# Attention in periods of six units, with one block of value products a group, in a kernel of hash attention and two mixers

## The chip, the cores and the metric

The kernel runs on 1 core of one Trainium2 chip. The metric is the device time of one execution in microseconds, the median of three runs. Engines are named TensorE (PE in the profile, with PEld for its weight loads), VectorE (DVE), ScalarE (ACT), GpSimd (POOL) and SyncE (SP, which only issues DMAs here).

## The reference, cut to what matters

Attention over 2 batches, 8 heads, 768 positions and 64 channels a head, in which a query sees only the keys of its hash bucket. Two mixing networks follow it; the change does not touch them.

```python
q_bits = (np.einsum('bhsd,dk->bhsk', q, proj) > 0).astype(np.int64)
k_bits = (np.einsum('bhsd,dk->bhsk', k, proj) > 0).astype(np.int64)
...
mask = q_bucket[:, :, :, None] == k_bucket[:, :, None, :]
scores = scale * np.matmul(q, k.transpose(0, 1, 3, 2))
scores = np.where(mask, scores, -1000000000.0)
scores = scores - np.max(scores, axis=-1, keepdims=True)
attn = np.exp(scores)
attn = attn / (np.sum(attn, axis=-1, keepdims=True) + 1e-09)
return np.matmul(attn, v).astype(np.float32)
```

## The kernel before

**Tiling.** A unit is 128 queries of one head against all 768 keys; there are 96 (`nunits`). A group is six units, three query tiles of each of the two heads of a head pair for half of the positions; there are 16. A pair is two groups; there are 8 (`npairs`). Units are numbered 0 to 95 through the whole kernel; where a unit is called 0 to 5 it is counted within its group.

**A unit's steps.** `scores` (L326, TensorE): four products of 128x384 into a tile `s` in PSUM, of which there are two. `peak` (L336, VectorE): moves `s` to SBUF (`p`, three buffers) and takes the row's maximum; `bias` (L344) scales it. `expo` (L354, ScalarE): the exponential in place, with its row sum. `transp` (L364, TensorE): 128x128 transposes, three to a half, into a PSUM tile `t`, of which there are three; `evac` (L370, ScalarE) copies each half into `PT`, where a group's six units come together. `move` is one half's transposes and copy.

**A group's steps.** `av` (L399, TensorE): two value products for one of six key tiles, so twelve a group, into the PSUM bank `obank`. `recip` (L379 to L382, VectorE, then four small DMAs of SP to DRAM): the reciprocals of the row sums. `spread` (L392, SP): two DMAs that broadcast them back. `finish` (L411, VectorE): their product with `obank`, into `XT`.

**Order.** Nothing reorders: each engine takes its instructions as the program writes them. The loop runs over 32 periods `p` of three units. A period has the scores of its first two units, the last transposes of the period before, six value products (`av3`, half a group, three periods back), then the scores of the third unit, and the transposes of the first two.

**Planned jobs.** `plan[(p, k)]` holds work that is strung between, with two slots `k` a period: hash bits of the next pair (`z`, L275 on TensorE, sign L282 on VectorE, scaling L289 and the differences L258 on GpSimd), loads, and the conversion of the mixers' weights (`weight_jobs`): magnitude L41 (ScalarE), clamp L44, shift L49, merge L55 (VectorE), first cast L71 (ScalarE), power L62, low part L65 (VectorE) and L76, L77 (GpSimd). In the last four periods the first mix of the next network is there too (L146 and L150 on VectorE, cast L121 on ScalarE, L122 on GpSimd). Behind the loop come the last value products between the first gate products (`r_group`, L176 on TensorE, sigmoid L214 on ScalarE, which needs another activation table than the exponential), and then the mixers.

Of the kernel before, what the change touches and what calls it, by code (L numbers as in the profile page):

```python
# [82 lines left out]
def hash_attention_moe_kernel(  # L83
# [134 lines left out]
    with tc.manual_schedule():  # L218
        attention(**env)
        mixers(**env)  # L220


def attention(tc, nc, mid, dram, ident, msc, omu, misc, cst_sb, pb, epsT, kq, vP, XT, TK0, wr, w_r, wk,
              w_k, w_v, ps_s, ps_t, obank, mix_jobs, r_group, tick, now, at_tick, plan_weight, wv, **_):
    PS = bass.MemoryType.PSUM
    with ExitStack() as ctx:
# [86 lines left out]
        nunits = npairs * 12  # L313
        P, PT, den, S_ps, C_sb, R = {}, {}, {}, {}, {}, {}

        def scores(i):
            g, u = divmod(i, 6)
            pp, half = divmod(g, 2)
            e, j = divmod(u, 3)
            t = TK[pp % 2][e]  # L320
            q0 = half * HS + 128 * j
            s = ps_s.tile([128, 2, 512], F32, tag="s", name="s")
            for n in range(2):
                w = t[:, 3 - n, q0:q0 + 128]
# [16 lines left out]
        def bias(i):  # L341
            c, m = C_sb[i]
            nb = at.tile([128, 1], F32, tag="nb", bufs=4, name="nb")
            nc.vector.tensor_scalar(nb, m, -0.125, None, op0=ALU.mult)  # L344
            C_sb[i] = (c, nb)

        def expo(i):
            g, u = divmod(i, 6)
            c, nb = C_sb.pop(i)
            if u == 0:  # L350
                den[g] = at.tile([128, 6], F32, tag="den", bufs=2, name="den")
                PT[g] = mid.tile([128, 2, 6, HS], F32, tag="PT", bufs=2, name="PT")
            c = c.rearrange("p c n -> p (c n)")
            nc.scalar.activation(  # L354
                c, c, AF.Exp, bias=nb, scale=0.125, accum_out=den[g][:, u:u + 1]
            )
            P[i] = c

        def transp(i, c):
            p = P[i] if c == 0 else P.pop(i)  # L360
            t = ps_t.tile([128, 512], F32, tag="t", name="t")
            for n in range(3):
                k0 = 128 * (3 * c + n)
                nc.tensor.transpose(t[:, 128 * n:128 * n + 128], p[:, k0:k0 + 128], ident)  # L364
            return t

        def evac(i, c, t):
            g, u = divmod(i, 6)
            e, j = divmod(u, 3)
            nc.scalar.copy(  # L370
                PT[g][:, e, 3 * c:3 * c + 3, 128 * j:128 * j + 128],
                t[:, :HS].rearrange("p (n q) -> p n q", n=3),
            )
# [3 lines left out]
        def recip(g):  # L377
            rc = rcs[g % 2]
            nc.vector.tensor_scalar_add(rc[:, 0:6], den.pop(g), 1e-9)  # L379
            nc.vector.reciprocal(rc[:, 0:6], rc[:, 0:6])  # L380
            rt = at.tile([128, 32], F32, tag="rt", bufs=2, name="rt")
            nc.vector.transpose(rt, rc)  # L382
            ds = dram.tile([6, 128], F32, tag="ds", name="ds")
            for n in range(4):
                nc.sync.dma_start(ds[:, 32 * n:32 * n + 32], rt[32 * n:32 * n + 6, :])
            R[g] = ds

        def spread(g):
            ds = R[g]
            R[g] = at.tile([128, 3, 128], F32, tag="rb", bufs=2, name="rb")  # L390
            for e in range(2):
                nc.sync.dma_start(  # L392
                    R[g][64 * e:64 * e + 64],
                    ds[3 * e:3 * e + 3].unsqueeze(0).to_broadcast([64, 3, 128]),
                )

        def av(g, kt):
            for e in range(2):
                nc.tensor.matmul(  # L399
                    obank[64 * e:64 * e + 64, :HS],  # L400
                    vt[g // 2][:, kt, e, :],
                    PT[g][:, e, kt, :],
                    start=(kt == 0),
                    stop=(kt == 5),
                )

        def finish(g):
            pp, half = divmod(g, 2)
            b, p = divmod(pp, NP)
            PT.pop(g)  # L410
            nc.vector.tensor_mul(  # L411
                XT[:, p, b, 1 + half * HS:1 + (half + 1) * HS],
                obank[:, :HS],
                R.pop(g).rearrange("p n q -> p (n q)"),
            )

        plan = {}
# [31 lines left out]
        np3 = nunits // 3  # L449
# [4 lines left out]
        for n, (dst, src, c, o) in enumerate(units):  # L454
            ld, jobs = weight_jobs(
                nc, mid, src[128 * c:128 * c + 128, o:o + 512],
                lambda dst=dst, c=c, o=o: (dst[:, 0, c, o:o + 512], dst[:, 1, c, o:o + 512]), nc.gpsimd,
            )
# [8 lines left out]
        for n, (which, c) in enumerate((w, c) for w in range(2) for c in range(4)):  # L467
            p0, k = 4 * (npairs - 1) + n // 2, n % 2
            jobs = mix_jobs(mid, 0, which, 4 * which, 2, nc.vector)
# [37 lines left out]
        nc.gpsimd.tensor_scalar(omu, msc[:, 34:42], -1.0, 1.0, op0=ALU.mult, op1=ALU.add)  # L507
        clear(1, nc.gpsimd)

        def av3(p):  # L510
            for n in range(3):
                av(p // 2, 3 * (p % 2) + n)

        def move(i, c):
            evac(i, c, transp(i, c))

        def score(i):
            peak(i)
            bias(i)

        for p in range(np3):
            a = 3 * p
            scores(a)
            scores(a + 1)
            score(a)
            if a:
                move(a - 1, 0)
            expo(a)
            if a:
                move(a - 1, 1)  # L530
            score(a + 1)
            expo(a + 1)
            if p >= 3:
                av3(p - 3)
            if p >= 2 and p % 2 == 0:
                recip(p // 2 - 1)
            for job in plan.pop((p, 0), ()):
                job()
            if p >= 3 and p % 2:
                spread((p - 3) // 2)  # L540
            if p >= np3 - 2:
                tick()
            scores(a + 2)
            move(a, 0)
            move(a, 1)
            score(a + 2)
            expo(a + 2)
            if p >= 4 and p % 2 == 0:
                finish((p - 4) // 2)
            move(a + 1, 0)  # L550
            move(a + 1, 1)
            for job in plan.pop((p, 1), ()):
                job()
            if p == np3 - 2:
                plan_wv()
            if p >= np3 - 2:
                tick()
        r_group(0, 0, mid)
        move(nunits - 1, 0)
        move(nunits - 1, 1)  # L560
        av3(np3 - 3)
        for k in range(2):
            for job in plan.pop((np3, k), ()):
                job()
        recip(np3 // 2 - 1)
        r_group(0, 1, mid)
        finish(np3 // 2 - 2)
        spread(np3 // 2 - 1)
        av3(np3 - 2)
        av3(np3 - 1)  # L570
        r_group(0, 2, mid)
        finish(np3 // 2 - 1)
        r_group(0, 3, mid)
        assert not plan, plan

# [304 lines left out]
```

## Time and profile before

| | |
|---|---|
| runs | 566.23 us median (565.66 to 567.29, three runs) |
| the profiled execution | 565.32 us; span 563.5 us |
| TensorE busy | 544.1 us (97%), 3188 products |
| TensorE weight loads | 464.9 us (82%) |
| VectorE busy | 378.4 us (67%) |
| ScalarE busy | 336.1 us (60%) |
| GpSimd busy | 143.2 us (25%) |
| granted TensorE clock | 0.999 of full over the span |

The attention takes the first 249 us of the span, the mixers the rest. Busy shares are means over both. A line of the timeline gives the start in us from the span's start, the duration in us, engine, line and operation, the tiles written and read, how many equal instructions in a row the line stands for, and in brackets how long the engine had been idle and what ended that. A product's own duration is longer than its distance to the next, since products overlap; paces are taken from start to start. Value products are recorded twice each, so that a block of twelve reads x24.

### The profile page before, as it was taken

The numbers are of one execution on the slowest core, as the hardware profiler recorded it, in microseconds if no ns is written. First come the engines' busy times: TensorE is split into PE (matmuls) and PEld (weight loads), VectorE is DVE, ScalarE is ACT, GpSimd is POOL, SyncE is SP. The second block draws the span as 40 slices with busy tenths as digits, with TensorE's granted clock in tenths as the row PEclk, the third lists the DMA queues.
The fourth block names the chain that finished last, engine by engine and source line by source line (L and its number), as shares of the span: only waits on it lengthen the run. The fifth ranks groups of instructions, "written<-read, shape, count | busy, mean of one in ns | idle before, by whom it ended". The sixth has DMA issues, their size and how long they took to land.

```text
span 563.5 us, 8998 instructions
## 1 busy us (share of the span) xinstructions
PE 544.1 (97%) x3188; PEld 464.9 (82%) x3188; DVE 378.4 (67%) x812; ACT 336.1 (60%) x718; POOL 143.2 (25%) x152
## 2 busy tenths in 40 slices
PE   7799999999999998899999999999999999999997
PEld 6667777666767666589899999999998989899896
DVE  6568886888688899749795674515997875353230
ACT  2788878788878878739753764708434452321121
POOL 5666665668475732200000000000110000000000
PEclk9999999999999999999999999999999999999999
DMA  8976497674949231111121211000573100001102
GB/s 173 237 185 132 140 174 180 131 198 78 214 99 244 66 101 45 40 56 71 37 76 39 66 47 38 1 1 0 177 239 90 57 28 1 2 19 38 56 20 94
DMA packets 20477, 51.96 MB, mean 92 GB/s; under 512 B 3840, under 2 KB 6864, under 8 KB 20432
## 3 DMA queue, kind: packets, MB, share of 16 engines
q1 hardware_dynamic: 13952, 31.71, 18.9%
q0 software_dynamic: 6336, 19.66, 17.2%
q8 instruction: 25, 0.41, 0.3%
q14 instruction: 20, 0.16, 0.1%
q10 hardware_dynamic: 144, 0.02, 0.1%
HBM read 47.08 MB, written 3.19 MB: 89 GB/s over the span
## 4 chain that ended last, share of the span: by engine, by line
PE 76%; DVE 12%; ACT 6%; DMA 3%; issue 2%; SPq 0%; POOL 0%; ACTq 0%; DVEq 0%; POOLq 0%
PE o L176 11%; PE o L399 8%; PE v L634 8%; PE s L326 8%; PE t L364 8%; PE k L176 8%; PE s L176 7%; PE w L176 5%; PE u L176 5%; DVE p L336 4%; PE o L634 3%; PE r L176 2%; DVE f L150 2%; ACT p L354 2%; DVE w_a L65 2%
## 5 line engine op out<-in xcount | busy, mean ns | idle before, releaser
L336 DVE TENSOR_SCALAR_CACHE_REDUCE p<-s 128x768 f32<-128x768 f32 x96 | 91.6, 954 | 27.0 <-PE s L326 22.3
L354 ACT ACTIVATE p<-p,nb 128x768 f32<-128x768 f32 x96 | 90.4, 942 | 18.8 <-DVE nb L344 18.4
L370 ACT COPY PT<-t 128x384 f32<-128x384 f32 x192 | 83.9, 476 | 21.5 <-PE t L364 20.6
L326 PE MATMUL s<-tk 128*128 128x384 f32 x384 | 84.7, 353 | 3.8 <-DVE p L336 2.2
L364 PE MATMUL t<-ident,p 128*128 128x128 f32 x576 | 79.7, 278 | 6.3 <-ACT p L354 3.7
L326 PEld LDWEIGHTS s<-tk 128*128 128x128 f32 x384 | 63.7, 188 | 23.8 <-issue 5.5
L364 PEld LDWEIGHTS t<-ident,p 128*128 128x128 f32 x576 | 65.1, 141 | 18.4 <-ACT p L354 8.0
L399 PE MATMUL o<-PT,v 128*64 128x384 f32 x384 | 68.8, 494 | 0.0
L176 PE MATMUL k<-tk,wk 128*128 128x384 f32 x336 | 59.6, 334 | 0.0
L258 POOL TENSOR_TENSOR tk<-x,tk 64x384 fp32r<-64x384 f32 x56 | 58.9, 1077 | 2.4 <-issue 1.5
L176 PEld LDWEIGHTS k<-tk,wk 128*128 128x128 f32 x336 | 58.4, 188 | 0.0
L634 PE MATMUL v<-k,wv 128*128 128x384 f32 x288 | 53.9, 335 | 0.6 <-DVE k L600 0.6
L634 PEld LDWEIGHTS v<-k,wv 128*128 128x128 f32 x288 | 50.3, 188 | 0.9 <-DVE k L600 0.9
L399 PEld LDWEIGHTS o<-PT,v 128*64 128x64 f32 x384 | 24.7, 136 | 28.5 <-issue 27.4
L693 POOL DMA_DIRECT2D wsp<-in_w_spT_dram x6 | 3.6, 612 | 169.0 <-DVE w_a L44 162.5
L176 PE MATMUL o<-wk,tk 128*128 128x512 f32 (+1 forms) x168 | 36.2, 374 | 0.0
L176 PEld LDWEIGHTS o<-wk,tk 128*128 128x128 f32 x168 | 30.0, 188 | 5.5
L615 ACT ACTIVATE kr<-k 128x384 f32<-128x384 f32 x28 | 13.6, 487 | 32.2 <-PE k L176 31.9
L600 DVE TENSOR_TENSOR k<-kt,k 128x384 fp32r<-128x384 f32 x32 | 17.8, 556 | 22.1 <-ACT k L618 22.0
L176 PE MATMUL r<-tk,wr 128*128 128x384 f32 x168 | 31.4, 339 | 0.8 <-ACT tk L121 0.5
L176 PEld LDWEIGHTS r<-tk,wr 128*128 128x128 f32 x168 | 29.0, 188 | 3.1 <-ACT tk L121 1.1
L176 PE MATMUL w<-wk,tk 128*128 128x512 f32 x132 | 30.7, 390 | 0.0
(108 smaller groups left out, 848.5 us busy)
## 6 DMA issues: line engine op xcount, KB each, us to landing
tk<-in_kq_dram POOLq DMA_DIRECT2D x32, 384.0 KB, 10.2
x<-in_kq_dram POOLq DMA_DIRECT2D x6, 768.0 KB, 8.0
w_raw<-in_w_k_dram SPq DMA_DIRECT2D x8, 512.0 KB
w_raw<-in_w_v_dram SPq DMA_DIRECT2D x8, 512.0 KB
w_raw<-in_w_in_dram SPq DMA_DIRECT2D x8, 512.0 KB
v<-in_vP_dram SPq DMA_DIRECT2D x8, 384.0 KB
rb<-ds SPq DMA_DIRECT2D x32, 96.0 KB
out_dram<-ot SPq DMA_DIRECT2D x11, 256.0 KB
```

The lines of the kernel that those rows point to most:

```text
L65: nc.vector.scalar_tensor_tensor(st["a"].bitcast(F32), st["raw"][:, :, 0], 2.0 ** -52, st["p"].bitcast(F32), op0=ALU.mult, op1=ALU.mult,)
L176: nc.tensor.matmul(o, a, x, start=(i == 0), stop=(i == len(seq) - 1))
L258: nc.gpsimd.tensor_sub(tk[l, 1 + 2 * t, o], raw[pp][l, t, o], tk[l, 2 * t, o])
L326: nc.tensor.matmul(s[:, c, :HS], w, t[:, n, c * HS:(c + 1) * HS], start=(n == 0), stop=(n == 1),)
L336: nc.vector.tensor_scalar(c, s[:, :, :HS], -BIG / 2, None, op0=ALU.max, op1=ALU.max, accum_out=m)
L354: nc.scalar.activation(c, c, AF.Exp, bias=nb, scale=0.125, accum_out=den[g][:, u:u + 1])
L364: nc.tensor.transpose(t[:, 128 * n:128 * n + 128], p[:, k0:k0 + 128], ident)
L370: nc.scalar.copy(PT[g][:, e, 3 * c:3 * c + 3, 128 * j:128 * j + 128], t[:, :HS].rearrange("p (n q) -> p n q", n=3),)
L399: nc.tensor.matmul(obank[64 * e:64 * e + 64, :HS], vt[g // 2][:, kt, e, :], PT[g][:, e, kt, :], start=(kt == 0), stop=(kt == 5),)
L600: later(lag, lambda: eng.tensor_sub(lo, src, hi))
L615: nc.scalar.activation(r, o[:, :HS], AF.Relu)
L634: nc.tensor.matmul(os[m][:, :HS], w, x, start=(c == 0 and k == 0), stop=(c == 7 and k == 2),)
```

## The change

The loop runs over the 16 groups instead of 32 periods. The twelve value products of a group stand in one block, behind the second unit of the group two later. Of each unit the transposes stand behind the scores of the unit two later; those of a group's last two units come between the first scores of the next group. Of the four job slots of a group, the first two are run together behind the second unit (behind the value block on TensorE), the third behind the fifth unit and the fourth behind the sixth. Behind the loop two units' transposes are left instead of one, and both remaining groups' value products are whole blocks.

```diff
-        for p in range(np3):
-            a = 3 * p
-            scores(a)
-            scores(a + 1)
-            score(a)
-            if a:
-                move(a - 1, 0)
-            expo(a)
-            if a:
-                move(a - 1, 1)
-            score(a + 1)
-            expo(a + 1)
-            if p >= 3:
-                av3(p - 3)
...
-            scores(a + 2)
-            move(a, 0)
-            move(a, 1)
-            score(a + 2)
-            expo(a + 2)
...
-            move(a + 1, 0)
-            move(a + 1, 1)
...
+        for g in range(ng):
+            a, p = 6 * g, 2 * g
+            last = g == ng - 1
+            for k in range(2):
+                scores(a + k)
+                score(a + k)
+                if g:
+                    both(a + k - 2)
+                expo(a + k)
+            if g >= 2:
+                for kt in range(6):
+                    av(g - 2, kt)
+            if g:
+                recip(g - 1)
+            jobs(p, 0)
+            jobs(p, 1)
...
+            scores(a + 2)
+            both(a)
+            score(a + 2)
+            expo(a + 2)
+            if g >= 2:
+                finish(g - 2)
+            scores(a + 3)
+            both(a + 1)
+            score(a + 3)
+            expo(a + 3)
+            if g:
+                spread(g - 1)
...
+            scores(a + 4)
+            both(a + 2)
+            score(a + 4)
+            expo(a + 4)
+            jobs(p + 1, 0)
...
+            scores(a + 5)
+            both(a + 3)
+            score(a + 5)
+            expo(a + 5)
+            jobs(p + 1, 1)
...
         r_group(0, 0, mid)
-        move(nunits - 1, 0)
-        move(nunits - 1, 1)
-        av3(np3 - 3)
...
+        both(nunits - 2)
+        both(nunits - 1)
+        for kt in range(6):
+            av(ng - 2, kt)
```

TensorE in the middle of the loop, one group of before, from a value block on (`s` scores, `t` transposes, `o` value products, `z` hash bits):

```order
L399 MATMUL o_70<-PT,v 64x384 x6
L326 MATMUL s<-tk_0_87 128x384 x4
L364 MATMUL t<-ident,p 128x128 x12
L326 MATMUL s<-tk_1_88 128x384 x8
L364 MATMUL t<-ident,p 128x128 x6
L399 MATMUL o_70<-PT,v 64x384 x6
L326 MATMUL s<-tk_1_88 128x384 x4
L364 MATMUL t<-ident,p 128x128 x12
L326 MATMUL s<-tk_0_77 128x384 x8
```

The same place now:

```order
L399 MATMUL o_70<-PT,v 64x384 x12
L326 MATMUL s<-tk_0_87 128x384 x4
L364 MATMUL t<-ident,p 128x128 x6
L326 MATMUL s<-tk_1_88 128x384 x4
L364 MATMUL t<-ident,p 128x128 x6
L326 MATMUL s<-tk_1_88 128x384 x4
L364 MATMUL t<-ident,p 128x128 x6
L326 MATMUL s<-tk_1_88 128x384 x4
```

Six value products behind every three units became twelve behind every six, and four score products alternate with one unit's six transposes.

ScalarE in group 7 before (`p` exponentials, `PT` copies of transposed halves, `wk` a weight's first cast, `w_a` a weight's magnitude):

```order
L370 COPY PT<-t 128x3x128
L354 ACTIVATE p,den<-p,nb 128x768
L71 CAST wk<-w_b 128x512
L41 ACTIVATE w_a<-w_raw 128x512
L370 COPY PT<-t 128x3x128 x2
L354 ACTIVATE p,den<-p,nb 128x768
L370 COPY PT<-t 128x3x128 x3
```

The same place now:

```order
L370 COPY PT<-t 128x3x128 x2
L354 ACTIVATE p,den<-p,nb 128x768
L71 CAST wk<-w_b 128x512
L41 ACTIVATE w_a<-w_raw 128x512
L370 COPY PT<-t 128x3x128 x2
L354 ACTIVATE p,den<-p,nb 128x768
L370 COPY PT<-t 128x3x128 x2
```

The two weight steps stay behind the fifth unit's exponential; the copies ahead of the next exponential are now both halves of the fourth unit, and the value block that stood close by is gone from there.

ScalarE at the end of the attention before (`rg` the first gate, L121 a cast of the mix):

```order
L354 ACTIVATE p,den<-p,nb 128x768
L370 COPY PT<-t 128x3x128 x2
L121 CAST tk_1_78<-f 128x384
L214 ACT_TABLE_LOAD
L214 ACTIVATE rg<-r 128x384
L370 COPY PT<-t 128x3x128 x2
```

And now:

```order
L354 ACTIVATE p,den<-p,nb 128x768
L121 CAST tk_1_78<-f 128x384
L214 ACT_TABLE_LOAD
L214 ACTIVATE rg<-r 128x384
L370 COPY PT<-t 128x3x128 x4
```

The copies of the unit before the last moved from ahead of the table load to behind the gate.

## Rows read from the trace of the kernel before

**Rows 1.** Windows, units 14-86: length, busy PE, PEld, DVE, ACT, POOL; clock.

```profile
40.70:205.60 164.90, 162.53 (x1059) 115.11 (x1057) 135.32 (x326) 138.47 (x312) 104.08 (x102) 1.00 0.66 147
```

**Rows 2.** Timeline of TensorE, a period and the hash bits after it.

```profile
93.11 2.16 PE L399 MATMUL o<-PT,v 128*64 128x384 f32 x12
...
96.00 1.61 PE L364 MATMUL t<-ident,p 128*128 128x128 f32 x12
97.36 1.64 PE L326 MATMUL s<-tk 128*128 128x384 f32 x8
98.84 0.82 PE L364 MATMUL t<-ident,p 128*128 128x128 f32 x6
99.59 2.16 PE L399 MATMUL o<-PT,v 128*64 128x384 f32 x12
101.67 0.85 PE L275 MATMUL z<-x,msc 128*32 128x384 f32 x8
102.46 0.96 PE L326 MATMUL s<-tk 128*128 128x384 f32 x4
```

**Rows 3.** Timeline of TensorE, scores of units 14 and 86.

```profile
40.69 0.98 PE L326 MATMUL s<-tk 128*128 128x384 f32 x4
...
205.58 0.96 PE L326 MATMUL s<-tk 128*128 128x384 f32 x4
```

**Rows 4.** Timeline of TensorE, end of the attention.

```profile
235.18 0.91 PE L364 MATMUL t<-ident,p 128*128 128x128 f32 x6 [0.81 <-ACT p L354]
236.02 2.16 PE L399 MATMUL o<-PT,v 128*64 128x384 f32 x12
...
240.41 4.09 PE L399 MATMUL o<-PT,v 128*64 128x384 f32 x24
244.43 4.43 PE L176 MATMUL r<-tk,wr 128*128 128x384 f32 x24
```

**Rows 5.** Timeline of ScalarE, end of the attention.

```profile
234.10 0.94 ACT L354 ACTIVATE p<-p,nb 128x768 f32<-128x768 f32 x1 [2.04 <-DVE nb L344]
...
235.04 0.84 ACT L370 COPY PT<-t 128x384 f32<-128x384 f32 x2
235.76 0.52 ACT L121 CAST tk<-f 128x384 fp32r<-128x384 f32 x1
236.30 1.28 ACT L214 ACT_TABLE_LOAD   x1
...
237.98 0.86 ACT L370 COPY PT<-t 128x384 f32<-128x384 f32 x2
```

**Rows 6.** Timeline of VectorE and ScalarE behind the scores at 102.46.

```profile
103.55 0.96 DVE L336 TENSOR_SCALAR_CACHE_REDUCE p<-s 128x768 f32<-128x768 f32 x1 [0.27 <-PE s L326]
...
104.80 0.94 ACT L354 ACTIVATE p<-p,nb 128x768 f32<-128x768 f32 x1 [0.15 <-DVE nb L344]
```

**Rows 7.** Timeline of ScalarE's weight steps, and transposes behind a copy.

```profile
116.72 0.61 ACT L71 CAST wk<-w_b 128x512 fp32r<-128x512 f32 x1
117.23 0.68 ACT L41 ACTIVATE w_a<-w_raw 128x512 f32<-128x512 f32 x1
117.81 0.84 ACT L370 COPY PT<-t 128x384 f32<-128x384 f32 x2
...
118.33 0.55 PE L364 MATMUL t<-ident,p 128*128 128x128 f32 x3 [0.36 <-ACT PT L370]
```

**Rows 8.** Source view (least/median/largest ns), two weight steps; timeline of VectorE, GpSimd.

```profile
L44 DVE TENSOR_SCALAR w_a<-w_a x14: 388/634/1354, 33.1 to 225.5; 128x512 f32<-128x512 f32 x14
...
L55 DVE SCALAR_TENSOR_TENSOR w_b<-w_raw,w_a x14: 649/688/1382, 36.4 to 229.5; 128x512 uint32<-128x512 uint32 x14
...
102.67 0.62 DVE L282 TENSOR_SCALAR zb<-z,msc 128x384 f32<-128x384 f32 x1 [0.91 <-PE z L275]
...
108.15 1.27 POOL L77 TENSOR_TENSOR wk<-w_b,w_a 128x512 fp32r<-128x512 f32 x1
...
108.49 1.21 DVE L44 TENSOR_SCALAR w_a<-w_a 128x512 f32<-128x512 f32 x1
```

More of the change, by code (lines that the diff above doesn't have):

```diff
@@ L508, in attention @@
         clear(1, nc.gpsimd)
-        def av3(p):
-            for n in range(3):
-                av(p // 2, 3 * (p % 2) + n)
         def move(i, c):
@@ L519, in score, with jobs @@
             bias(i)
-        for p in range(np3):
-            a = 3 * p
-            scores(a)
-            scores(a + 1)
-            score(a)
-            if a:
-                move(a - 1, 0)
-            expo(a)
-            if a:
-                move(a - 1, 1)
-            score(a + 1)
-            expo(a + 1)
-            if p >= 3:
-                av3(p - 3)
-            if p >= 2 and p % 2 == 0:
-                recip(p // 2 - 1)
-            for job in plan.pop((p, 0), ()):
-                job()
-            if p >= 3 and p % 2:
-                spread((p - 3) // 2)
-            if p >= np3 - 2:
+        def jobs(p, k):
+            for job in plan.pop((p, k), ()):
+                job()
@@ new lines, in both @@
+        def both(i):
+            move(i, 0)
+            move(i, 1)
+        ng = nunits // 6
+        for g in range(ng):
[14 more added lines that the diff above has]
+            jobs(p, 1)
+            if last:
@@ L542, in attention @@
                 tick()
             scores(a + 2)
-            move(a, 0)
-            move(a, 1)
+            both(a)
             score(a + 2)
             expo(a + 2)
-            if p >= 4 and p % 2 == 0:
-                finish((p - 4) // 2)
-            move(a + 1, 0)
-            move(a + 1, 1)
-            for job in plan.pop((p, 1), ()):
-                job()
-            if p == np3 - 2:
-                plan_wv()
-            if p >= np3 - 2:
+            if g >= 2:
+                finish(g - 2)
@@ new lines, in attention @@
+            scores(a + 3)
[4 more added lines that the diff above has]
+                spread(g - 1)
+            if last:
+                plan_wv()
+                tick()
+            scores(a + 4)
[3 more added lines that the diff above has]
+            jobs(p + 1, 0)
+            if last:
+                tick()
+            scores(a + 5)
+            both(a + 3)
+            score(a + 5)
+            expo(a + 5)
@@ L557, in attention @@
+            jobs(p + 1, 1)
+            if last:
                 tick()
         r_group(0, 0, mid)
-        move(nunits - 1, 0)
-        move(nunits - 1, 1)
-        av3(np3 - 3)
[L562 to L565, printed above, removed]
+        both(nunits - 2)
+        both(nunits - 1)
+        for kt in range(6):
+            av(ng - 2, kt)
+        jobs(np3, 0)
+        jobs(np3, 1)
+        recip(ng - 1)
         r_group(0, 1, mid)
-        finish(np3 // 2 - 2)
@@ L568, in attention @@
-        spread(np3 // 2 - 1)
-        av3(np3 - 2)
-        av3(np3 - 1)
+        finish(ng - 2)
+        spread(ng - 1)
+        for kt in range(6):
+            av(ng - 1, kt)
         r_group(0, 2, mid)
-        finish(np3 // 2 - 1)
+        finish(ng - 1)
         r_group(0, 3, mid)
```

## The prediction, made before the changed kernel ran

> **What bounds the kernel now.** I read first the windows view of the stretch that the change rewrites [rows 1]. Between the scores of unit 14 and those of unit 86, twelve groups, TensorE's matmul row is busy 162.53 of 164.90 us, ScalarE 138.47 and VectorE 135.32. So three engines are nearly full, and whether TensorE's time is worth anything depends on what stands next to it. The timeline of one clean period of before [rows 2] gives TensorE's own pace: 99.59 - 93.11 = 6.48 us for three units, two such periods 12.96 us a group, and in every second group the hash-bit products add 102.46 - 101.67 = 0.79 us. Twelve groups at that pace are 12 x 12.96 + 6 x 0.79 = 160.3 us; measured are 205.58 - 40.69 = 164.9 us [rows 3]. Only 4.6 us of waits are there to be won, plus what the new order saves in TensorE work.
>
> **What the change saves on TensorE.** Two blocks of value products of 101.67 - 99.59 = 2.08 us become one of 244.43 - 240.41 = 4.02 us [rows 2, 4]: 0.14 us less. Scores and transposes alternate in smaller runs. Eight score products took 98.84 - 97.36 = 1.48 us, so four take 0.74; twelve transposes took 97.36 - 96.00 = 1.36 us, so six take 0.68 at most (a wait for a copy is in it). A unit is thus 1.42 us. I see no price for a switch between the two kinds; bounds are 0 and the 0.07 us by which six transposes ahead of a value block (99.59 - 98.84 = 0.75) are above 0.68; I take 0.
>
> **What now sets a group: ScalarE.** Before, a value block came after every three units and ScalarE caught up under it. Now six units follow each other, and ScalarE needs more than TensorE's 1.42 us for each. Its pace: exponential at 234.10, two copies at 235.04, next step at 235.76, so 1.66 us [rows 5]. With units 0 to 5 of a group and time 0 at the start of the scores of unit 2 (the first after the value block), step by step. exp(2) starts at 2.34 (scores 102.46, peak 103.55, exponential 104.80) [rows 2, 6]. exp(5) starts at 2.34 + 3 x 1.66 = 7.32: ScalarE runs from the one to the other without a gap, each exponential behind the copies of the unit two before. The transposes of unit 5 start 1.08 later (235.18 - 234.10) [rows 4, 5], at 8.40. TensorE alone would be there at 0.74 + 5 x 1.42 = 7.84, so it waits. The value block follows 0.84 later (236.02 - 235.18), at 9.24, and the next scores of a unit 2 at 9.24 + 4.02 = 13.26. So a plain group costs 13.26 us where before's clean one costs 12.96. The hash-bit products (0.79) fall into TensorE's waits and come free, or nearly. Twelve groups: 159.1 us, 5.8 less than measured before.
>
> **What comes on top.** ScalarE's weight steps (the absolute value, L41, and the first cast, L71) stand where the plan puts them: behind unit 1 they are covered by the value block, behind unit 4 or 5 they lie on the chain above. By the order, four absolute values and six casts of these twelve groups lie there. An absolute value costs 117.81 - 117.23 = 0.58, a cast 117.23 - 116.72 = 0.51 [rows 7]: 4 x 0.58 + 6 x 0.51 = 5.4 us. Before, most of them fell into ScalarE's idle time.
>
> VectorE's weight steps behind unit 4 delay the peak of unit 5. Its peak 4 starts at 2.84 + 1.09 = 3.93 and with its bias takes 1.1, until 5.03; peak 5 must start by 7.32 - 1.25 = 6.07 (1.25 = 104.80 - 103.55). That leaves about 1.0 us. Two steps lie there in most groups, by the medians a clamp 0.63 or a merge 0.69 with a shift that I take at a clamp's least, 0.39: 1.0 to 1.1 us [rows 8], about the room. In the six groups with hash bits the sign step (0.62) comes too and 0.65 to 0.75 is late; in two of them ScalarE's steps there are longer and cover it. Four such groups 2.8 us, the others 0.3: 3.1 us. Bounds: 2.1 us if all steps take their least, nothing if the peaks come earlier too (1.42 is an upper value); 3.1 + 11 x 0.7 = 10.8 us if a clamp's worst (1.35 against 0.63) stood in all eleven groups that have such steps. I take 3.1, by the medians. The middle comes to -5.8 + 5.4 + 3.1 = +2.7 us.
>
> The other moved steps cost nothing by my reading. Reciprocals (VectorE) and the two slots of jobs behind unit 1 lie under the value block, where VectorE has about 4 us. The reciprocals' four small DMAs and the two broadcasts (SP), the weight loads (SP) and those of keys and queries (POOL) keep their order and are asked for no less than a period before use; a late broadcast would hold the finishing product on VectorE, and the peak of unit 3 behind it. Up to unit 14 both orders have done the same work, with ScalarE as the limit, and I put no difference there.
>
> **The end**, from the scores of unit 86 to the last pair of gate products: before 244.43 - 205.58 = 38.85 us [rows 3, 4]. New: group 14 has an absolute value and two casts of the mix behind units 4 and 5, 13.26 + 1.4 = 14.66. In group 15 the nine VectorE steps of the two merged slots (some 0.55 each, between a clamp's least and a merge's median) and the reciprocals need 5.5 us against some 4.2 until peak 2: 1.3 late; five more behind unit 4 need 2.8 against 1.0: 1.8 late. The last exponential then starts at 14.66 + 1.3 + 7.32 + 1.8 = 25.1. Before, the transposes of unit 94 were out of the way by then; now they stand behind the first gate products with those of unit 95, there are three transpose banks for four halves, and ScalarE reaches the first copy only after a cast, the 1.28 us table load and the gate: 0.94 + (237.98 - 235.76) = 3.16 after the exponential [rows 5]. The last half is free 0.52 later (118.33 - 117.81 [rows 7]), the value block 0.42 after that: 29.2. Then 4.02 + gates 2.31 (240.41 - 236.02 - 2.08) + 4.02 gives 39.5, so +0.7 us; -2.0 if VectorE is never late, +2.4 if its steps are slow.
>
> **Sum.** +2.7 + 0.7 = +3.4 us on the profiled 565.32 us (span 563.5): 568.7. The median of the runs, 566.23, is 0.9 above that one; on it the forecast is **569.6 us**, slower by 0.6%. What a measurement of this kernel can tell from no change is about 0.3%, 1.7 us.
>
> **Rivals.** The first: VectorE is in time everywhere: its weight steps behind unit 4 and the merged slots of group 15 end before the peaks are due. It turns on whether the 1.0 us of room is rather 1.6. Then the middle is -5.8 + 5.4 = -0.4, the end -2.0: 563.8 us, not slower. For it: the least times, and that in groups with hash bits POOL is idle until the sign step. Against it: the medians. 20%.
>
> The second: VectorE is blocked by POOL. A clamp took 1.21 us at 108.49 while POOL was at a weight step from 108.15 to 109.42, against a median of 0.63 [rows 8]. If most of the eleven steps meet POOL, some 6 us come on top: about 576. 20%. The Trainium skill, SBUF — State Buffer, section "Who interferes with whom", says that the pair of ports shared by VectorE and GpSimd is an exclusive lock, and that the later of two such steps waits for the whole of the first. By that rule a step loses up to a full POOL step wherever POOL runs; the 1.21 agrees, the median says that it is not the usual case.
>
> The third: TensorE stays the limit and the saving is kept: a group at 7.84 + 0.75 + 4.02 = 12.61, with hash bits 13.40: twelve take 156.1, -8.8 us, the weight steps hide, the end gives -2: 555. It needs ScalarE under 1.5 us a unit, which the rows at 1.66 speak against; TensorE's matmul row, 162.53 of 164.90, speaks for it. 8%. The Trainium skill, Trace Analysis, section "Identifying the Most-Contended Engine", holds that the matmul row isn't a good measure for TensorE, and that weight-load occupancy is; that is 115.11 of 164.90 [rows 1], under ScalarE's 138.47. By it ScalarE is the one to relieve, and this change gives it nothing.
>
> **Chances and range.** Forecast 52%, rivals 20, 20 and 8%. Faster by over 0.3%: rival 3 and most of rival 1, 23%. Within 0.3%: the rest of rival 1 and the low edge of the forecast, 17%. Slower: 60%. The range runs from rival 1 to just short of rival 2's mean: 563.5 to 575.5 us.
>
> **What would show it.** In the new trace, plain groups of 13.2 to 13.4 us from one value block to the next, with TensorE waiting for the exponential (L354) or a copy (L370) ahead of transposes (L364); ScalarE's gaps only under the value blocks; absolute values and casts behind units 4 and 5 lengthening their groups one for one; a wait of 2 us or more before the last transposes, behind the table load. Wrong would be: groups of 12.6 us with TensorE never waiting (rival 3), or waits of TensorE traced to VectorE's weight steps in most groups (rival 2). The forecast falls if ScalarE shows gaps between exp(2) and exp(5).

## The result, and the profile of the changed kernel

The changed kernel takes 571.76 us (median of 5 runs, 568.73 to 572.15) against 565.66 us (564.56 to 567.29) before: a ratio of 1.0099, interval 1.0083 to 1.0116. It is 6.1 us slower where 3.4 were forecast. The profiled execution took 571.88 us (span 570.1) against 565.32. Its 6.56 us lie in three places: 0.73 up to the scores of unit 14 (now at 41.42), 1.91 from there to those of unit 86 (208.21; 166.79 us in place of 164.88), and 3.92 from there to the first product of the next stage (47.05 in place of 43.13).

The windows of the changed kernel answer to [rows 1], columns as there (PE, PEld, DVE, ACT, POOL busy; then the granted clock). The first is the stretch from unit 14 to unit 86; the others are at the end.

```profile
41.40:208.20 166.80, 161.86 (x1058) 114.08 (x1056) 137.20 (x329) 135.78 (x310) 103.20 (x103) 1.00 0.66 148
226.10:228.10 2.00, 0.02 (x1) 0.03 (x1) 1.86 (x5) 0.00 (x0) 0.11 (x1) 1.00 0.68 265
229.20:232.40 3.20, 3.02 (x12) 2.92 (x13) 3.06 (x9) 3.20 (x9) 0.00 (x0) 0.50 0.00 0
239.40:242.60 3.20, 3.20 (x14) 1.22 (x12) 0.00 (x0) 0.58 (x2) 0.99 (x1) 0.50 0.43 69
```

In the second window TensorE stands idle for 2 us at full clock; about 1 us behind it, it runs at a granted clock of 0.50, which is 1.2 GHz of 2.4, and from 239.4 to 242.6 it does so again.

A group without ScalarE's weight steps outside the block, TensorE and ScalarE (answers to [rows 2, 5]):

```profile
166.97 0.97 PE L326 MATMUL s<-tk 128*128 128x384 f32 x4
...
175.38 0.91 PE L364 MATMUL t<-ident,p 128*128 128x128 f32 x6
176.22 1.19 PE L399 MATMUL o<-PT,v 128*64 128x384 f32 x6
```

```profile
168.31 0.86 ACT L370 COPY PT<-t 128x384 f32<-128x384 f32 x2 [1.81 <-PE t L364]
169.23 0.94 ACT L354 ACTIVATE p<-p,nb 128x768 f32<-128x768 f32 x1
...
174.30 0.94 ACT L354 ACTIVATE p<-p,nb 128x768 f32<-128x768 f32 x1
```

From the scores of unit 2 (166.97) to exp(2), at 169.23, are 2.26 us, three more units take 5.07 (174.30; 3 x 1.66 = 4.98 and 0.08 of lateness of VectorE ahead of exp(5)), the last transposes start 1.08 behind exp(5), the block 0.84 behind these. ScalarE's only gap (1.81) is under the block. A group with a cast and an absolute value behind unit 4:

```profile
103.46 0.96 ACT L354 ACTIVATE p<-p,nb 128x768 f32<-128x768 f32 x1
...
104.39 0.63 ACT L71 CAST wk<-w_b 128x512 fp32r<-128x512 f32 x1
104.90 0.69 ACT L41 ACTIVATE w_a<-w_raw 128x512 f32<-128x512 f32 x1
...
106.20 0.97 ACT L354 ACTIVATE p<-p,nb 128x768 f32<-128x768 f32 x1
```

Here one exponential follows the other after 2.74 us and not 1.66: the two steps stand in the chain with their full 1.08.

The worst group of the middle (15.06 us), GpSimd under its block, and VectorE beside it:

```profile
49.13 6.56 POOL L258 TENSOR_TENSOR tk<-x,tk 64x384 fp32r<-64x384 f32 x6
55.66 1.27 POOL L76 TENSOR_TENSOR w_b<-w_b,wr 128x512 f32<-128x512 f32 x1
...
54.76 2.47 DVE L44 TENSOR_SCALAR w_a<-w_a 128x512 f32<-128x512 f32 x1
57.14 0.95 DVE L336 TENSOR_SCALAR_CACHE_REDUCE p<-s 128x768 f32<-128x768 f32 x1
```

The scores of its unit 2 began at 54.81; the peak starts 2.33 later, not 1.0, behind a clamp that took 2.47 us.

The end, TensorE, ScalarE and VectorE (answers to [rows 4, 5]):

```profile
222.83 0.97 PE L326 MATMUL s<-tk 128*128 128x384 f32 x4
...
228.08 0.98 PE L326 MATMUL s<-tk 128*128 128x384 f32 x4 [1.99 <-DVE p L336]
...
238.48 0.55 PE L364 MATMUL t<-ident,p 128*128 128x128 f32 x3 [2.03 <-ACT PT L370]
238.95 5.78 PE L399 MATMUL o<-PT,v 128*64 128x384 f32 x24
244.66 2.38 PE L176 MATMUL r<-tk,wr 128*128 128x384 f32 x12
246.97 4.09 PE L399 MATMUL o<-PT,v 128*64 128x384 f32 x24
```

```profile
234.82 0.94 ACT L354 ACTIVATE p<-p,nb 128x768 f32<-128x768 f32 x1 [0.97 <-DVE nb L344]
...
236.27 1.28 ACT L214 ACT_TABLE_LOAD   x1
...
237.95 1.62 ACT L370 COPY PT<-t 128x384 f32<-128x384 f32 x4
```

```profile
223.09 1.47 DVE L150 SCALAR_TENSOR_TENSOR f<-XT,msc,d 128x384 f32<-128x384 f32 x1
...
227.06 0.95 DVE L336 TENSOR_SCALAR_CACHE_REDUCE p<-s 128x768 f32<-128x768 f32 x1
```

GpSimd beside these steps:

```profile
223.13 1.01 POOL L122 TENSOR_TENSOR tk<-f,tk 128x384 fp32r<-128x384 f32 x1 [4.06 <-ACT tk L121]
225.18 1.03 POOL L122 TENSOR_TENSOR tk<-f,tk 128x384 fp32r<-128x384 f32 x1 [1.04 <-ACT tk L121]
```

The peak of unit 92 starts 4.23 us after its scores (222.83); TensorE waits 1.99. Two of VectorE's mix steps ahead of that peak are long where GpSimd has a mix step of its own (L122): L150 (223.09, 1.47 us) ends 0.42 behind GpSimd's end at 224.14, and L146 (225.27, 1.15 us) 0.21 behind 226.21. The last half of the transposes waits for the first copy behind the table load, and the block behind it takes 244.66 - 238.95 = 5.71 us where the next one takes 4.02.

### The profile page after: what moved, and what is told of

Read it like the earlier page. It is cut to its first block, busy times and chain, and to the rows that moved or that the text cites. A ratio compares the mean times of both kernels' runs of the same rounds, so it can differ in the third digit from the quotient of the medians.

```text
span 570.1 us, 9030 instructions
## 1 busy us (share of the span) xinstructions
PE 547.8 (96%) x3188; PEld 466.9 (82%) x3188; DVE 378.4 (66%) x812; ACT 333.2 (58%) x718; POOL 142.7 (25%) x152
## 3 DMA queue, kind: packets, MB, share of 16 engines
q0 software_dynamic: 6336, 19.66, 16.6%
## 4 chain that ended last, share of the span: by engine, by line
PE 69%; ACT 15%; DVE 10%; issue 3%; DMA 2%; SPq 0%; ACTq 0%; DVEq 0%; POOLq 0%
PE o L176 11%; PE o L399 9%; PE v L649 8%; PE k L176 8%; PE s L176 7%; ACT p L354 6%; PE w L176 5%; PE u L176 5%; PE s L326 5%; PE t L364 5%; ACT PT L370 4%; DVE p L336 3%; PE o L649 3%; PE r L176 2%; DVE f L150 1%
## 5 line engine op out<-in xcount | busy, mean ns | idle before, releaser
L354 ACT ACTIVATE p<-p,nb 128x768 f32<-128x768 f32 x96 | 92.0, 958 | 9.0 <-DVE nb L344 8.0
L326 PE MATMUL s<-tk 128*128 128x384 f32 x384 | 92.8, 364 | 3.8 <-DVE p L336 2.7
L364 PE MATMUL t<-ident,p 128*128 128x128 f32 x576 | 85.7, 282 | 9.3 <-ACT PT L370 6.5
L364 PEld LDWEIGHTS t<-ident,p 128*128 128x128 f32 x576 | 66.6, 143 | 26.9 <-ACT p L354 12.7
L399 PE MATMUL o<-PT,v 128*64 128x384 f32 x384 | 67.1, 500 | 0.0
L258 POOL TENSOR_TENSOR tk<-x,tk 64x384 fp32r<-64x384 f32 x56 | 57.0, 1045 | 2.0 <-issue 1.0
L399 PEld LDWEIGHTS o<-PT,v 128*64 128x64 f32 x384 | 26.7, 139 | 32.5 <-issue 32.4
```

Source lines behind the costliest of these rows:

```text
L258: nc.gpsimd.tensor_sub(tk[l, 1 + 2 * t, o], raw[pp][l, t, o], tk[l, 2 * t, o])
L326: nc.tensor.matmul(s[:, c, :HS], w, t[:, n, c * HS:(c + 1) * HS], start=(n == 0), stop=(n == 1),)
L354: nc.scalar.activation(c, c, AF.Exp, bias=nb, scale=0.125, accum_out=den[g][:, u:u + 1])
L399: nc.tensor.matmul(obank[64 * e:64 * e + 64, :HS], vt[g // 2][:, kt, e, :], PT[g][:, e, kt, :], start=(kt == 0), stop=(kt == 5),)
```

## The experiments

The theory was that of the prediction: outside the value block a group is one chain through ScalarE, so steps of ScalarE there cost their full time and steps under the block cost nothing. The rivals: VectorE, or VectorE held up by GpSimd, sets the time; or the merged block alone does. In each part "the middle" is the time from the scores of unit 14 to those of unit 86 (before 164.88, changed 166.79), "the end" from there to the first k product (43.13 and 47.05).

**The parts of the change.** First the kernel before with the merged block alone.

```diff
-            if p >= 3:
-                av3(p - 3)
+            if p >= 4 and p % 2 == 0:
+                av3(p - 4)
+                av3(p - 3)
...
+        av3(np3 - 4)
         av3(np3 - 3)
```

> The kernel before with the other part alone: its periods of three units and its order of scores and transposes, but the twelve value products of a group in one block in every second period. Theory: ScalarE's chain of six units between blocks sets the group as in the changed kernel, 13.2 us and its weight steps on top: slower than before by 1 to 6 us, 567 to 572. Rival (the block saves its 0.14 us of TensorE a group and costs nothing): 563.5 to 565.5.

574.48 us (572.87 to 576.47), ratio 1.0161 (1.0133 to 1.0190). The middle is 171.52, 6.6 longer than before; the end, 43.14, is untouched. Its waits:

```profile
ACT PT L370 <- PE t L364: 29.2, 19, 2.9
PE t L364 <- ACT p L354: 5.7, 15, 0.7
```

(Engine, line and releaser; us in total, times, longest.) The time is above the theory's 567 to 572 and far from the rival. ScalarE stands idle under the block up to 2.9 us, and TensorE waits for exponentials behind it: the merged block costs 6.6 us in the old order. The changed kernel, which has the alternation and the moved job slots besides, gets most of it back (166.79); which of the two does that, this run doesn't separate. Next the changed kernel with two half blocks, one behind unit 1 and one behind unit 4.

```diff
-                for kt in range(6):
+                for kt in range(3, 6):
                     av(g - 2, kt)
...
             expo(a + 4)
+            if g:
+                for kt in range(3):
+                    av(g - 1, kt)
             jobs(p + 1, 0)
```

> The changed kernel, but with six value products behind unit 1 and six behind unit 4 (the first half of the group before), instead of twelve behind unit 1; scores and transposes alternate as in the changed kernel. Theory (the one long block is what hurts: ScalarE's six units in a row outlast TensorE's, and what lies behind units 4 and 5 is uncovered): groups fall to TensorE's own pace, 6 x 1.36 + 2 x 2.08 = 12.3 us and 0.8 in every second, so unit 14 to unit 86 takes 152 to 158 us instead of 166.8, and the time is 559 to 564, below the kernel before. Rival (alternating scores and transposes in smaller runs is what costs): within 2 us of the changed kernel, 570 to 572.

575.93 us, ratio 1.0186 (1.0171 to 1.0202): both missed. Five groups fell to 12.71 to 13.49, near the pace expected, but others took 15.7, 16.6 and 17.5; in the two longest the granted clock also fell to half for 3.4 us (from 59.2 and from 117.3).

```profile
DVE zb L282 <- PE z L275: 7.5, 6, 1.7
```

The sign step waits on VectorE for hash-bit products that stand behind the half block, and the peaks behind it are late (scores wait for them 5.5 us in all). So the edit brought a wait of its own and did not test the theory. The same with that mended: periods of three units, the slot's jobs ahead of the half block, its second part behind the third unit again, and the end as in the first experiment under **The end**.

```diff
+        for p in range(np3):
+            a = 3 * p
+            for k in range(2):
+                scores(a + k)
+                score(a + k)
+                if p:
+                    both(a + k - 2)
+                expo(a + k)
...
+            jobs(p, 0)
+            if p >= 3:
+                half(p - 3)
...
+            scores(a + 2)
+            both(a)
+            score(a + 2)
+            expo(a + 2)
...
+            jobs(p, 1)
```

> The changed kernel's alternation of scores and transposes, but in periods of three units with half a value block (three key tiles) each, the other work of a slot issued ahead of the half block and not behind it, the slots' second halves back behind the third unit, and the second-last unit's transposes ahead of the first gate products. Theory: a clean half group falls to 6.4 us (12.7 a group, as in three clean groups of the other kernel with half blocks), the sign no longer stands behind a half block, and VectorE's work is spread again as before: the stretch from unit 14 to unit 86 takes 160 to 163 us, the end 43, the time 560 to 563. Rival: with half the block to cover it the weight steps on ScalarE and the clamps on VectorE are late again: 570 to 576.

565.43 us (563.32 to 568.57, 10 runs), ratio 1.0000 (0.9982 to 1.0017). The middle is 164.08, not 160 to 163: one group at 12.71, the rest 13.2 to 14.7. Better than 570, short of 560 to 563, and no gain on the kernel before; against the changed kernel the half blocks, with the slots put back, are worth 2.7 us of the middle. Its waits name VectorE:

```profile
ACT p L354 <- DVE nb L344: 9.0, 17, 1.3
```

**ScalarE's room.** Two absolute values over 128 x 160 on a scratch tile, in twelve groups, behind unit 4; then the same behind exp(1), under the block.

```diff
             expo(a + 4)
+            if 2 <= g <= 13:
+                for _ in range(2):
+                    nc.scalar.activation(scr, scr, AF.Abs)
```

> The changed kernel with two more ScalarE instructions (Abs over 128 x 160, in place on a scratch tile, together about 0.6 us by the 0.58 us of an Abs over 128 x 512) behind exp(4) of each of the twelve groups 2 to 13. Theory of the prediction: outside the value block a group is one chain through ScalarE, so each of them lengthens its group one for one: 12 x 0.6 = 7 us, 571.8 becomes 577 to 580, and the distance between the scores of unit 14 and unit 86 grows from 166.8 to about 174. Rival: ScalarE has room between two units there too (it is busy 136 of 167 us), the time stays within 2 us of 571.8.

> The changed kernel with the same two ScalarE instructions, in the same twelve groups, but behind exp(1), where TensorE starts the value block. Theory of the prediction: ScalarE waits there for the block's end (its copies wait 26.8 us in twelve places, up to 2.9 us each), so they cost 0 to 1 us: 571 to 573. Rival: what stands on ScalarE costs the same everywhere: 577 to 580 as behind unit 4.

Behind unit 4: 576.82 us (575.07 to 579.60), middle 172.23, +5.4. Under the block: 571.13 us (570.06 to 575.19), middle 166.51, -0.3. Behind unit 4 the group of the two instructions (x count, busy us, mean ns), and ScalarE's wait for the transposes behind the block:

```profile
L567 ACT ACTIVATE scr<-scr 128x160 f32<-128x160 f32 x24 | 8.2, 340 | 0.4
```

```profile
ACT PT L370 <- PE t L364: 26.4, 12, 2.9
```

The same wait with them under the block:

```profile
ACT PT L370 <- PE t L364: 20.3, 12, 2.3
```

Same work, 5.7 us apart by its place alone: under the block it came out of ScalarE's idle time, which fell by 6 us. Behind unit 4 the step from exp(4) to exp(5) is 2.28 us in each plain group, against 1.66: +0.62. Twelve times that is 7.4; of the 2 us less than that, 0.5 are group 3, whose late peak came 0.46 us sooner, and the rest are groups where VectorE was late at the same place, so that ScalarE had waited anyway. The time is just under the 577 to 580 expected for that reason; that the place decides is what the theory said, and the 0.62 fixes the price.

**Moving the weight steps.** First all steps of the odd periods moved to the next group's block.

```diff
-                at_slot(p0 + dp, k, job)
+                odd = (p0 + dp) % 2
+                at_slot(p0 + dp + odd, 0 if odd else k, job)
```

> The changed kernel with one edit: the weight steps that its plan puts behind units 4 and 5 of a group (ScalarE's absolute values and first casts, VectorE's clamps, shifts, merges) go behind unit 1 of the next group, under the value block. Theory (a group is set by ScalarE's chain from the first exponential behind the value block, so a step on it lengthens the group one for one, and under the block it is free): plain groups stay at 13.2 to 13.4 us, the long ones (13.8 to 15.1 now) come down to that, the twelve groups from unit 14 to unit 86 take 159 to 161 us instead of 166.8, the time falls by 6 to 7.5 us to about 565. Rival (the steps cost as much under the block, because VectorE is then late for the first peak behind it, as it was in group 15): the groups stay at 13.9 us in the mean, 570 to 572.

577.04 us, ratio 1.0204 (1.0180 to 1.0229), middle 170.6: both missed. Five groups take 13.33 to 13.46, the others 13.56 to 15.9.

```profile
ACT wk L71 <- DVE w_b L55: 9.6, 4, 3.6
DVE w_a L44 <- ACT w_a L41: 5.5, 5, 2.1
```

Now a cast stands in the same slot as the merge that makes its input: ScalarE waits for VectorE up to 3.6 us with its copies behind, and VectorE's clamp waits for ScalarE. GpSimd is in it too: around the end of a block at 140.53 shift and merge take 1.39 and 1.38 us beside its steps, and the peak of unit 2 starts 3.66 behind its scores, not 1.0. That is the rival's mechanism, larger than its numbers. The place was free, the dependence was not. So next: one weight a group, ScalarE's steps under the blocks with their inputs made a group earlier, VectorE's one behind each of units 2 to 5.

```diff
-            p0 = 2 + 9 * n // 4
+            p0 = 2 + 2 * n
...
+            where = ((0, 0), (0, 2), (0, 3), (1, 0), (2, 0), (1, 1), (2, 0), (2, 1))
...
+            jobs(p, 2)
...
+            jobs(p, 3)
```

> The changed kernel with the weight conversion dealt out anew: one weight a group from group 1 on, its two ScalarE steps (magnitude, cast) always under a value block, its VectorE steps one behind each of units 2, 3, 4 and 5 and one under the next block. No operation is added or left out. Theory of the prediction, as the runs so far leave it (a group is 13.2 to 13.4 us when neither a weight step stands on ScalarE outside the block nor VectorE comes late): twelve groups take 159 to 162 us in place of 166.8, the end stays at 47, the time is 565 to 567. Rival: the lateness comes from VectorE's sum of work and from GpSimd beside it wherever the steps stand: 166 to 168 between unit 14 and unit 86, 570 to 573.

573.10 us (569.12 to 575.40), middle 167.43: the rival. No weight step of ScalarE is left outside a block, 5.4 us of chain are gone, and VectorE took them back. The groups alternate between 13.67 and 14.4; the last, without steps on VectorE, takes 13.22. GpSimd and VectorE in a long one:

```profile
87.09 2.15 POOL L258 TENSOR_TENSOR tk<-x,tk 64x384 fp32r<-64x384 f32 x2
...
86.43 0.99 DVE L44 TENSOR_SCALAR w_a<-w_a 128x512 f32<-128x512 f32 x1
87.33 0.94 DVE L336 TENSOR_SCALAR_CACHE_REDUCE p<-s 128x768 f32<-128x768 f32 x1
...
88.39 1.14 DVE L49 TENSOR_SCALAR w_a<-w_a 128x512 uint32<-128x512 uint32 x1
```

A peak and its bias take 1.06 us (87.33 to 88.39) of a unit of 1.66, so VectorE has 0.6 us between two peaks. A clamp of 0.42 fits; one of 0.99 beside GpSimd does not, and the exponentials come 0.68 and 0.35 late. Last, all of ScalarE's and VectorE's steps under the blocks, one weight a group, with the end of the next experiment.

```diff
+            p0 = 4 + 2 * n
...
+            where = ((0, 2), (0, 0), (0, 0), (0, 0), (2, 0), (0, 0), (2, 0), (2, 1))
...
+                if k:
+                    jobs(p, 2)
                 expo(a + k)
```

> The changed kernel with the weight conversion dealt out as one weight a group from group 2 on, and all of it that ScalarE and VectorE do put under the value blocks: magnitude ahead of exp(1), clamp, shift, merge and power on VectorE under that block, cast and low part under the next; and the second-last unit's transposes ahead of the first gate products. No operation is added or left out. Theory, as the kernel with one weight step behind each unit leaves it: between two units of 1.66 us VectorE has some 0.5 us over after a peak and its bias (1.08 us), so one locked step or a step beside the sign lengthens a group, while under a block it waits up to 3.4 us and ScalarE up to 1.8 us: the steps there (0.42 + 0.42 + 0.68 + 0.42 + 0.65 us and the reciprocals) fit, groups take 13.2 to 13.6 us, the stretch from unit 14 to unit 86 takes 159 to 163 us, the end 43 to 44.5, the time is 560 to 564. Rival: the chain magnitude, clamp, shift, merge, power is drawn out by GpSimd beside it (the clamp 2.47 us in group 3 of the changed kernel) past the peak of unit 2: groups 14 to 15, the stretch 166 to 170, the time 567 to 571.

585.67 us, ratio 1.0355 (1.0329 to 1.0381). From group 4 on every second group takes 13.33 to 13.36, as the theory has it, and every other one 17.4, far over the rival's 14 to 15. VectorE under the block of a short group, and of a long one with GpSimd beside it:

```profile
101.20 0.43 DVE L44 TENSOR_SCALAR w_a<-w_a 128x512 f32<-128x512 f32 x1 [0.29 <-ACT w_a L41]
101.66 0.43 DVE L49 TENSOR_SCALAR w_a<-w_a 128x512 uint32<-128x512 uint32 x1
102.12 0.69 DVE L55 SCALAR_TENSOR_TENSOR w_b<-w_raw,w_a 128x512 uint32<-128x512 uint32 x1
...
114.74 1.23 DVE L44 TENSOR_SCALAR w_a<-w_a 128x512 f32<-128x512 f32 x1
116.00 2.35 DVE L49 TENSOR_SCALAR w_a<-w_a 128x512 uint32<-128x512 uint32 x1
118.38 1.66 DVE L55 SCALAR_TENSOR_TENSOR w_b<-w_raw,w_a 128x512 uint32<-128x512 uint32 x1
...
121.09 0.95 DVE L336 TENSOR_SCALAR_CACHE_REDUCE p<-s 128x768 f32<-128x768 f32 x1
```

```profile
112.30 4.52 POOL L258 TENSOR_TENSOR tk<-x,tk 64x384 fp32r<-64x384 f32 x4
116.78 1.28 POOL L76 TENSOR_TENSOR w_b<-w_b,wk 128x512 f32<-128x512 f32 x1
118.14 1.35 POOL L77 TENSOR_TENSOR wk<-w_b,w_a 128x512 fp32r<-128x512 f32 x1
```

The shift ends (118.35) 0.3 us behind the end of GpSimd's subtraction of 116.78 (118.06), the merge (120.04) 0.55 behind that of its addition (119.49), each at about its own time behind GpSimd's step: clamp, shift and merge take 5.24 us where they took 1.55. TensorE then waits 2.65 for the peak, which starts 4.62 behind its scores in place of 1.0: 3.6 of the 4.1 us by which this group is longer than a short one. Behind that wait the granted clock falls to half, here and in the four other groups of 17.4, and goes with the other 0.5 (columns as in the windows above):

```profile
123.50:126.80 3.30, 3.30 (x14) 3.21 (x15) 1.75 (x7) 3.20 (x8) 1.08 (x3) 0.50 0.86 243
```

The Trainium skill, SBUF — State Buffer, section "Who interferes with whom", has VectorE and GpSimd share a pair of ports under an exclusive lock, and exempts a step that also writes its accumulator; these rows agree on both, since the peak at 87.33 above took its 0.94 beside GpSimd.

**The end.** The transposes of unit 94 ahead of the first gate products.

```diff
-        r_group(0, 0, mid)
         both(nunits - 2)
+        r_group(0, 0, mid)
         both(nunits - 1)
```

> The changed kernel with one edit at the end: the transposes and copies of unit 94 stand ahead of the first gate products, as those of the last unit but one did before, and only unit 95's behind them. Theory: the 2.03 us in which TensorE waits for a copy behind the table load go, and with that idle stretch the fall of the granted clock behind it, which made the next value block 5.7 us instead of 4.0: together -3.5 us, about 568. If the clock falls all the same: -2 us. Rival (the end is set by VectorE's late steps alone, the copies' place is covered): no change, 571 to 572.

567.15 us (566.56 to 567.67), ratio 1.0035 (1.0020 to 1.0050), as expected: the end 43.44 in place of 47.05, no 2 us wait behind the table load, and blocks of 4.02. So of the 3.6 us, 1.7 are the clock's. In the profile the middle (167.02) did not move, and unit 14 came at 39.96, which the edit can't have done. Then the second slot of the last two even periods behind the third unit again.

```diff
             jobs(p, 0)
-            jobs(p, 1)
+            if g < ng - 2:
+                jobs(p, 1)
...
+            if g >= ng - 2:
+                jobs(p, 1)
```

> The changed kernel with the second slot of the last two even periods moved back from under the value block to behind the third unit, as in the kernel before; nothing else. In the changed kernel the peak of unit 92 started 4.24 us after its scores and unit 94 waited 1.99 us. Theory: that lateness is the sum of two slots' VectorE work under one block; with one of them behind unit 2 the wait before the scores of unit 94 falls under 0.8 us, the end (scores of unit 86 to the first k product) goes from 47.05 to 44 to 45.5, the time to 569 to 570.5. Rival: the work only becomes late elsewhere (the same work between the same units): the end stays at 46.5 to 47.5.

572.77 us (571.30 to 574.34), the end 46.32: the rival, nearly, and only by the clock. The 2.03 us wait behind the table load is there as before, but no fall of the clock follows it in this trace, and the block takes 4.02 in place of 5.71; without these 1.7 us the end would be about 48.0, 1 us longer than the changed kernel's (an estimate from these numbers). The wait ahead of the scores of unit 94 is gone, and one ahead of unit 95 has come:

```profile
230.20 0.97 PE L326 MATMUL s<-tk 128*128 128x384 f32 x4 [1.44 <-DVE p L336]
```

Group 14 went from 14.61 to 15.47 with the work put between its units. The three edits together:

> The changed kernel with three edits together: the weight conversion dealt out as one weight a group with its ScalarE steps under the blocks, the second slot of the last two even periods behind the third unit, and the second-last unit's transposes ahead of the first gate products. If the terms are apart from one another, the middle takes 159 to 162 us and the end 42.5 to 43.5: 560 to 563, below both kernels. Rival (VectorE late wherever the steps stand): 566 to 569.

569.56 us (568.13 to 573.43), ratio 1.0076 (1.0047 to 1.0105). Middle 167.47 and end 44.51: the rival. The middle is that of the weights dealt out, and the end is 1.1 us longer than with unit 94's transposes moved alone; 0.9 of that is group 14, which takes 15.47 here too.

**The clock.** Ten products into the unused output bank fill the idle stretch in the first group.

```diff
+            if g == 0:
+                warm(10)
             jobs(p + 1, 0)
```

> The changed kernel with ten 128 x 128 products into the unused output bank in the first group, ahead of the hash-bit products behind unit 4, where TensorE had been idle 2.5 us (17.95 to 20.45) and its granted clock then fell to half (20.9 to 24.3). Theory: the idle stretch is what the clock falls after; with it filled the dip at 21 is gone and the scores of unit 14 start 1 to 1.3 us earlier (41.42 becomes 40.1 to 40.4): 570.5. Rival: the dip comes wherever it comes (the kernel before idles 2.58 us at the same place without one): the start of unit 14 stays at 41.4 or moves by the products' own time.

The median, 571.30 us, can't be told from 571.76, but the head can be read. The window from 21 to 23 us and the hash-bit products, changed:

```profile
21.00:23.00 2.00, 2.00 (x9) 1.38 (x6) 0.62 (x1) 0.00 (x0) 0.49 (x1) 0.50 1.22 207
```

```profile
20.45 1.15 PE L275 MATMUL z<-x,msc 128*32 128x384 f32 x8 [2.50 <-ACT p L354]
```

And filled (the ten products read x20, recorded twice each):

```profile
21.00:23.00 2.00, 2.00 (x19) 1.59 (x12) 1.13 (x2) 0.28 (x1) 0.63 (x1) 1.00 1.28 194
```

```profile
17.91 2.40 PE L267 MATMUL o<-ident 128*128 128x128 f32 x20
```

In the filled kernel unit 14 starts at 40.69, where it did before the change, and the slow window is gone. The two slow stretches at the end remain. These are single traces: in two others with the same work up to unit 14 it starts at 39.96 (unit 94's transposes moved; half clock from 11.1 to 17.9) and at 41.84 (the last slots apart; half clock from 16.3 to 19.7). So the head differs by more than 0.73 us from one execution to the next.

## Why the prediction was right, and where its terms were off

**A group is set by ScalarE: right, to 0.1 us.** Forecast 2.34 + 4.98 + 1.92 + 4.02 = 13.26; measured, step by step at the usual value, 2.26 + 4.98 + 1.94 + 4.02 = 13.20, and the groups without lengthening take 13.22 to 13.39. The hash-bit products came free. Against 164.9 that is 12 x 13.20 = 158.4, -6.5 (forecast -5.8).

**ScalarE's weight steps: right.** The four absolute values and six casts lengthened the steps from exp(4) to exp(5) by 0.56, 1.09, 1.07 and 0.56, and those from exp(5) to the block by 0.54, 0.51, 0.50 and 0.54: 5.4 us, as forecast. The experiment with extra absolute values shows that place, and not work, makes the price.

**VectorE's lateness in the middle: the sum right (2.8 against 3.1), the place half wrong.** 1.5 us are small delays, 0.08 to 0.50 each, most behind unit 4. The other 1.32 are one clamp under the block of group 3. "The other moved steps cost nothing by my reading" failed there: the reading counted VectorE's time under the block and not GpSimd's beside it. It is the second rival's mechanism in one group of the middle; the runs that moved more steps under the block or between the peaks paid it in every second group.

**Up to unit 14: 0 forecast, 0.73 measured.** The work was the same, but the granted clock was at half after the idle stretch at 20. In the trace that filled it there was no fall and no 0.73; since the head of single traces differs by more than that with the same work, that the 0.73 is the price of this fall is likely, not shown.

**The end: forecast +0.7, measured +3.9 in all.** The chain behind the last exponential was right: 3.66 to the last half (forecast 3.68), 4.13 to the block (4.1). Group 14 was too (14.61, forecast 14.66). Two terms were mis-sized. VectorE in group 15 was 3.1 late at peak 2 and 1.5 behind unit 4, not 1.3 and 1.8: mix steps taken at 0.55 took 1.47 (223.09) and 1.15, each beside a step of GpSimd, which the sum had left out here as well. That is 1.5 us. And the block ran at half clock for most of its time, 5.71 for 4.02: 1.7 us, for which the sum had no term. From the scores of unit 86 to the last r pair the two make 3.2 of the 3.3 us that were missing (42.78 measured, 39.5 forecast).

**The sum.** The forecast of +3.4 is 3.2 us short of the profile's 6.56: 0.8 too much in the middle, 0.7 and 3.2 too little in the head and at the end. That the kernel got slower rests on the middle and on the chain at the end, which held. No term of the sum had the falls of the clock: 1.7 us in the block, and the 0.73 of the head if it is theirs.

**The rivals.** The first (VectorE in time everywhere) is excluded by the late peaks in the middle and at the end. The second (VectorE held up by GpSimd) was no general state of the changed kernel: it cost one group of the middle 1.32 us and group 15 the 1.5. But it is what a better plan meets. The third (TensorE the limit) is excluded by the chain of ScalarE. What stays open: whether a plan that keeps GpSimd's pieces away from the blocks would keep groups at 13.3 throughout; that wasn't tried. No kernel here beat the one before by more than a measurement can tell.

## What to carry to other kernels

Merging two blocks of TensorE work saves next to nothing there (0.14 us) and takes away a place where the other engines catch up: price each step of the next-limiting engine by whether it stands under such a block or in the chain. When steps are moved under the block, look at what they depend on in the same slot, and at GpSimd beside VectorE: here the same three VectorE steps took 1.55 us alone and 5.24 beside it. And order the last unit's work ahead of whatever loads a table or waits: that one line was worth 3.6 us here, 1.7 of them because the clock then did not fall.

## What the runs showed of the hardware that was not expected

The granted clock fell from 2.4 to 1.2 GHz within the kernel, behind idle stretches of TensorE of 2.50, 1.99 and 2.03 us, and rose again with work going on. It is not regular: the kernel before idled 2.58 us at the same place of the head at full clock throughout, and the kernel with unit 94's transposes moved idled 2.17 us until 226.75 without a fall. In the traces of the experiments it fell behind waits as short as 1.44 us (ahead of 230.20, with the last slots apart) and behind all five waits of 2.6 us with the weights' steps under the blocks. The wait of 2.0 us behind the table load stands in seven traces, and in six of them a slow stretch goes with it: the value block behind it took 5.3 to 6.4 us there, and 4.02 with the last slots apart. In the five runs of the changed kernel four had a mean clock of 0.991 (571.1 to 572.2 us) and one 0.997 (568.73 us); the 3 us between them are about what the slow stretches cost in the profile (some 0.7 at the head, 1.7 in the block). What decides whether such a stretch is followed by a fall, these runs don't settle.
